# Bucketed attention and a mixture of experts on one core: 2048 instead of 16384 bytes per partition reserved for descriptors of GpSimd's DMAs

## The chip, the cores and the metric

The kernel runs on one core of a Trainium2 chip. The metric is the device time of one execution in microseconds (us), the median of several runs. A profiled execution has a span, from its first to its last recorded instruction, and a time of its own, which is a little longer.

## What is computed

Attention over 4 batches, 8 heads, 768 tokens of 64 channels, in which a query sees only the keys of its own bucket (6 sign bits of a projection), and then a mixture of 8 experts in which every token goes to the expert with the largest logit:

```python
mask = q_bucket[:, :, :, None] == k_bucket[:, :, None, :]
scores = np.where(mask, scale * np.matmul(q, k.transpose(0, 1, 3, 2)), -1000000000.0)
attn = np.exp(scores - np.max(scores, axis=-1, keepdims=True))
x = (attn / (attn.sum(-1, keepdims=True) + 1e-09)) @ v      # to 3072 rows of 512
e_idx = np.argmax(x @ w_gate, axis=1)
for e in range(8):
    mask = e_idx == e
    h = np.maximum(x[mask] @ w1[e], 0.0)                     # 512 to 1024
    out[mask] = gate_w[mask, None] * eom[mask, e, None] * (h @ w2[e])
```

All data are float32.

## The kernel before

**Attention, to about 480 us.** 192 steps, each a tile of 128 queries of one head against its 768 keys: scores on TensorE (L484), their minimum on VectorE (L488), the exponential on ScalarE (L496), the division by the row's sum on GpSimd (L506), a transpose on TensorE (L517), its eviction (L518), the product with the values (L528). The output goes to the DRAM tensor x_dram. Routing (the expert of each token and its place in a table) runs between the steps.

**Experts, from about 480 us.** The experts come in order of their load. An expert takes up to 512 tokens, in chunks of at most 128. While expert r is computed, GpSimd collects the rows of experts r+1 and r+2 by indirect DMAs: `gather` (L239) takes 128 rows of 2 KB, `gather_part` (L271) takes 128 pieces of 512 B, so that a chunk needs up to four. VectorE transposes a chunk (L280), GpSimd rounds it (L283, tile xh), VectorE forms the rest (L284, xlo). TensorE multiplies with three products for each float32 product (`product`, L297): `up` into hidden units, then `down` or, for experts with at most 384 tokens, `all_rows`. ScalarE evicts the hidden units (L307, hh), VectorE their rest (L308, hl), which frees the PSUM tile, of which there are two (ps_s).

**The way out.** `send` (L310) lets ScalarE scale a chunk of results into the tile yo (L313), of which there are two, and GpSimd scatter its rows to the output:

```python
yo = mp.tile([CH, DM], F32, name="yo", bufs=2)
nc.scalar.activation(yo[0:n], py[0:n], AF.Copy, scale=tacc[0:n, 1, r, a:a + 1])
nc.gpsimd.indirect_dma_start(
...
    in_=yo[0:n], in_offset=None, bounds_check=NTOK - 1, oob_is_err=False)
```

The order of the work on all compute engines is written out by hand (`tc.manual_schedule`): GpSimd's queue holds the gathers, the scatters and the roundings in one order, and ScalarE's queue the yo of one expert between the hh of others.

**The end.** After the last expert a number of further rounds is computed (L965 to L975), for tokens over an expert's limit; here it is 0, and the body of `tc.If(nr > 0)` (L976) is skipped. [...] The end of the tile context (profile line 1057) makes every engine's queue DRAIN, waits for all at a barrier, clears the semaphores and waits at a second barrier. In all, GpSimd issues 112 DMAs (8 by L239, 75 by L271, 29 by L314), the first at 416.6 us.

**The reservation.** The program object made at L1050 reserves, at the start of every SBUF partition, a part for the descriptors of GpSimd's DMAs, 16384 bytes if nothing is given. Tiles of pools on the left side are placed from its end on, those of pools on the right side (hp and ep) from the other end of the partition.

## Time and profile before

| | |
|---|---|
| time, median of 3 runs | 811.73 us (811.72 to 812.19) |
| time of the profiled execution | 811.82 us |
| its span | 810.1 us |
| TensorE matmul busy | 773.2 us, 95% of the span |
| GpSimd (POOL) busy | 378.4 us, 47% |
| mean granted TensorE clock | 0.986 of full speed |

A page and views of a trace are read as follows. Engines are PE (TensorE matmul), PEld (its weight loads), DVE (VectorE), ACT (ScalarE), POOL (GpSimd) and SP; a "q" behind a name is the engine's instruction queue, whose waits, branches and drains don't count as busy time. L314 is line 314 of the kernel. In a view of one line, a row gives how often an operation ran, its duration in ns (min/median/max), and when the first and the last began. In the order of time, a row gives start, duration, engine and operation, and in brackets how long the engine sat idle before it and what ended that.

### The profile page before, as it was taken

What the parts mean: (1) busy time and instruction counts of PE and PEld (TensorE: products, weight loads), DVE (VectorE), ACT (ScalarE), POOL (GpSimd) and SP (SyncE); (2) the same over time, 40 slices, a digit from 0 to 9 for tenths busy, and PEclk for the clock granted to TensorE, in tenths of its full rate; (3) what the DMA queues carried; (4) which work ended last, traced back from release to release, by engine and by line L of the source; (5) the groups of instructions that cost most, each with busy time, mean ns of one, the idle gap of its engine ahead of it and who ended that gap; (6) DMA issues with size and microseconds to landing.
All of it is one profiled execution on the core that took longest, in us unless ns stands there. A gap on an engine that the chain in (4) does not pass through costs nothing. (4 is left out here: it accounts for less than half of the span.)

```text
span 810.1 us, 13652 instructions
## 1 busy us (share of the span) xinstructions
PE 773.2 (95%) x4656; PEld 604.5 (75%) x4656; DVE 475.0 (59%) x1036; ACT 459.3 (57%) x934; POOL 378.4 (47%) x415
## 2 busy tenths in 40 slices
PE   5899999999999989999999999999999999999992
PEld 3666776666776667766667758888999999988881
DVE  5566576686667776766877637246254546455330
ACT  5767777767777677777677741243343444434320
POOL 5535444435444434443366773373436454564100
PEclk8999999999999999999999999999999999999997
DMA  3543645543564454565374432363444453645300
GB/s 122 126 119 74 146 98 121 120 123 70 136 144 87 103 140 84 121 142 131 64 204 104 115 78 46 114 222 122 137 151 146 150 175 122 222 145 182 140 15 24
DMA packets 84895, 98.94 MB, mean 122 GB/s; under 512 B 58047, under 2 KB 59535, under 8 KB 84816
## 3 DMA queue, kind: packets, MB, share of 16 engines
q1 hardware_dynamic: 79472, 84.66, 40.0%
q0 software_dynamic: 5200, 13.31, 4.9%
q8 instruction: 39, 0.64, 0.3%
q14 instruction: 40, 0.33, 0.1%
q10 hardware_dynamic: 144, 0.01, 0.0%
HBM read 59.48 MB, written 13.11 MB: 90 GB/s over the span
## 5 line engine op out<-in xcount | busy, mean ns | idle before, releaser
L506 POOL TENSOR_SCALAR sc<-sc,rsum 128x768 f32<-128x768 f32 x192 | 179.8, 948 | 234.5 <-DVE rsum L504 127.2
L488 DVE TENSOR_SCALAR_CACHE_REDUCE sc<-ps_s 128x768 f32<-128x768 f32 x192 | 183.2, 956 | 112.2 <-PE ps_s L484 104.2
L518 ACT COPY pts<-ps_t 128x384 f32<-128x384 f32 x384 | 164.4, 480 | 98.2 <-PE ps_t L517 97.4
L496 ACT ACTIVATE sc<-sc,mn 128x768 f32<-128x768 f32 x192 | 181.3, 944 | 25.8 <-DVE sc L488 16.8
L517 PE MATMUL ps_t<-ident,sc 128*128 128x128 f32 x1152 | 160.2, 275 | 6.4 <-POOL sc L506 3.8
L517 PEld LDWEIGHTS ps_t<-ident,sc 128*128 128x128 f32 x1152 | 137.3, 141 | 19.7 <-issue 6.7
L528 PE MATMUL ps_a<-pts,vt 128*64 128x384 f32 x768 | 146.4, 503 | 0.0
L484 PE MATMUL ps_s<-xr,xl 128*128 128x384 f32 x384 | 118.0, 389 | 6.2 <-DVE sc L488 3.5
L484 PEld LDWEIGHTS ps_s<-xr,xl 128*128 128x128 f32 x384 | 58.5, 192 | 78.0 <-issue 37.2
L484 PE MATMUL ps_s<-yr,yl 76*128 76x384 f32 x384 | 101.1, 344 | 0.4 <-DMA yl<-bt 0.4
L308 DVE SCALAR_TENSOR_TENSOR hl<-ps_s,hh 128x256 fp32r<-128x256 f32 (+8 forms) x40 | 33.9, 848 | 112.0 <-ACT hh L307 112.0
L297 PE MATMUL ps_s<-xh,w1h 128*128 128x256 f32 (+7 forms) x288 | 97.1, 337 | 2.0 <-DVE hl L308 1.3
L297 PE MATMUL ps_s<-xlo,w1h 128*128 128x256 f32 (+7 forms) x288 | 95.3, 331 | 0.0
L297 PE MATMUL ps_s<-xh,w1l 128*128 128x256 f32 (+7 forms) x288 | 95.2, 331 | 0.0
L271 POOL DMA_INDIRECT xq<-x_dram,idx x75 | 82.7, 1103 | 21.6 <-issue 20.7
L528 PEld LDWEIGHTS ps_a<-pts,vt 128*64 128x64 f32 x768 | 47.2, 137 | 51.6 <-issue 49.8
L314 POOL DMA_INDIRECT out_dram<-yo,sid x29 | 32.0, 1105 | 114.5 <-ACT yo L313 62.7
L307 ACT ACTIVATE hh<-ps_s 128x256 fp32r<-128x256 f32 (+8 forms) x40 | 29.0, 726 | 93.0 <-PE ps_s L297 93.0
L484 PEld LDWEIGHTS ps_s<-yr,yl 76*128 76x128 f32 x384 | 71.1, 192 | 1.1 <-DMA yl<-bt 0.7
L297 PEld LDWEIGHTS ps_s<-xh,w1h 128*128 128x128 f32 x288 | 54.1, 188 | 5.0 <-DVE hl L308 1.8
L297 PEld LDWEIGHTS ps_s<-xlo,w1h 128*128 128x128 f32 x288 | 54.1, 188 | 1.2
L297 PEld LDWEIGHTS ps_s<-xh,w1l 128*128 128x128 f32 x288 | 54.1, 188 | 1.1
(199 smaller groups left out, 1002.2 us busy)
## 6 DMA issues: line engine op xcount, KB each, us to landing
w_raw<-in_w_dram SPq DMA_DIRECT2D x36, 512.0 KB
qk<-in_qkT_dram SPq DMA_DIRECT2D x32, 384.0 KB
xh<-in_w_dram SPq DMA_DIRECT2D x14, 512.0 KB
xlo<-in_w_dram SPq DMA_DIRECT2D x14, 512.0 KB
vt<-in_v_dram SPq DMA_DIRECT2D x16, 384.0 KB
xr<-xl SPq DMA_DIRECT2D x30, 192.0 KB
yr<-xl SPq DMA_DIRECT2D x30, 192.0 KB
xr<-yl SPq DMA_DIRECT2D x30, 192.0 KB
```

Of the source, the lines that this page charges most:

```text
L271: nc.gpsimd.indirect_dma_start(out=xq[:, k * P:(k + 1) * P], out_offset=None, in_=x_dram.rearrange("n (a f) -> (n a) f", a=NB32), in_offse ...
L297: nc.tensor.matmul(ps, l, r, start=first and k == 0, stop=last and k == len(pairs) - 1)
L307: nc.scalar.activation(hh, ph, AF.Relu)
L308: return lambda: nc.vector.scalar_tensor_tensor(hl, ph, 0.0, f32(hh), ALU.max, ALU.subtract)
L314: nc.gpsimd.indirect_dma_start(out=out[:, :], out_offset=bass.IndirectOffsetOnAxis(ap=sid[0:n, r, a:a + 1], axis=0), in_=yo[0:n], in_offse ...
L484: nc.tensor.matmul(ss[:, n, 0:HS], l[0:k, qs], r[0:k, n * HS:(n + 1) * HS], start=first, stop=not first)
L488: nc.vector.tensor_scalar(sc, ss[:, :, 0:HS], MASKED, None, ALU.min, ALU.min, accum_out=mn)
L496: nc.scalar.activation(pr, pr, AF.Exp, bias=mn, scale=-1.0, accum_out=sums[s // GROUP][:, k:k + 1])
L506: nc.gpsimd.tensor_scalar(live[s0 + k], live[s0 + k], rs[:, k:k + 1], 0.0, ALU.mult, ALU.add)
L517: nc.tensor.transpose(tr[:, c], pr[:, (3 * h + c) * P:(3 * h + c + 1) * P], ident)
L518: nc.scalar.copy(pts[:, 3 * h:3 * h + 3, t * P:(t + 1) * P], tr)
L528: nc.tensor.matmul(st["av"][j * D:(j + 1) * D], st["v"][:, j, c], blocks[hb][j][:, c], start=(c == 0), stop=(c == NT - 1))
```

## The change

The reservation is given as 2048 bytes per partition.

```diff
-    nc = bacc.Bacc("TRN2", target_bir_lowering=False, num_devices=1)
+    nc = bacc.Bacc("TRN2", target_bir_lowering=False, num_devices=1, dynamic_dma_scratch_size=2048)
```

Nothing else differs. The instructions of all five engines, their order and their waits are the same. Of the tiles in SBUF, those on the left side lie 14336 bytes lower in every partition; those on the right side stay where they were.

## Rows read from the trace of the kernel before

**Rows 1.** The page: busy time of each engine, share, instructions.

```profile
PE 773.2 (95%) x4656; PEld 604.5 (75%) x4656; DVE 475.0 (59%) x1036; ACT 459.3 (57%) x934; POOL 378.4 (47%) x415
```

**Rows 2.** Busy time by stretch, first row the columns.

```profile
core 0: us, PE busy (x) PEld busy (x) DVE busy (x) ACT busy (x) POOL busy (x), PEclk, DMA share, GB/s
...
715.00:745.00 30.00, 28.72 (x149) 25.80 (x148) 15.22 (x16) 9.96 (x13) 17.93 (x17) 1.00 0.47 159
...
765.00:800.00 35.00, 30.50 (x158) 26.39 (x156) 8.29 (x8) 8.87 (x11) 3.22 (x4) 1.00 0.08 27
800.00:810.00 10.00, 0.00 (x0) 0.00 (x0) 0.00 (x0) 0.00 (x0) 0.00 (x0) 0.54 0.00 0
```

**Rows 3.** Line 1057: count, duration ns min/median/max, first and last start us.

```profile
L1057 POOLq EVENT_SEMAPHORE  x4: 17/17/17, 809.3 to 810.0; - x4
L1057 POOLq DRAIN  x3: 40/107/9226, 800.1 to 809.8; - x3
L1057 SPq DRAIN  x3: 7/7/13, 800.7 to 809.6; - x3
...
L1057 ACTq DRAIN  x2: 8/8/8, 799.0 to 809.6; - x2
```

**Rows 4.** Line 976, the skipped branch, same columns.

```profile
L976 POOLq INC_SWDGE_SEM  x1: 2418/2418/2418, 797.6 to 797.6; - x1
```

**Rows 5.** Line 1050, the program's start, same columns.

```profile
L1050 POOLq INC_SWDGE_SEM  x1: 31/31/31, 0.2 to 0.2; - x1
...
L1050 POOLq DRAIN  x1: 176/176/176, 0.4 to 0.4; - x1
```

**Rows 6.** Line 314 from 796 us on: the last scatter, and its landing.

```profile
L314 POOL DMA_INDIRECT out_dram<-yo,sid x1: 918/918/918, 796.5 to 796.5; - x1
...
DMA to landing us min/median/max: 2.8/2.8/2.8
```

**Rows 7.** Lines 239, 271, 314 over the span; the landing is line 271's.

```profile
L239 POOL DMA_INDIRECT xg<-x_dram,gid x8: 946/970/1397, 416.6 to 524.6; - x8
...
L271 POOL DMA_INDIRECT xq<-x_dram,idx x75: 940/946/1971, 525.8 to 734.4; - x75
...
DMA to landing us min/median/max: 2.4/3.2/7.0
...
L314 POOL DMA_INDIRECT out_dram<-yo,sid x29: 874/1005/1854, 506.6 to 796.5; - x29
```

**Rows 8.** POOL in order of time, from 716 us to 734 us.

```profile
716.42 0.87 POOL L314 DMA_INDIRECT out_dram<-yo,sid  x1 [1.24 <-issue]
...
731.80 0.94 POOL L271 DMA_INDIRECT xq<-x_dram,idx  x1 [0.30 <-issue]
733.05 1.03 POOL L314 DMA_INDIRECT out_dram<-yo,sid  x1 [0.30 <-issue]
```

**Rows 9.** ACT, DVE and PE in order of time, about 735 us to 739 us.

```profile
735.89 0.69 ACT L313 ACTIVATE yo<-ps_m,tacc 128x512 f32<-128x512 f32 x1 [11.75 <-DMA out_dram<-yo,sid]
736.48 0.78 ACT L307 ACTIVATE hh<-ps_s 128x736 fp32r<-128x736 f32 x1
...
737.29 0.93 DVE L308 SCALAR_TENSOR_TENSOR hl<-ps_s,hh 128x736 fp32r<-128x736 f32 x1 [11.60 <-ACT hh L307]
...
738.27 0.44 PE L297 MATMUL ps_s<-xh,w1h 128*128 128x368 f32 x1 [1.28 <-DVE hl L308]
```

**Rows 10.** POOL: its 15th DMA, and the first instructions after three runs of gathers.

```profile
530.82 0.94 POOL L271 DMA_INDIRECT xq<-x_dram,idx  x1 [0.30 <-issue]
...
557.60 0.61 POOL L283 TENSOR_SCALAR xh<-xt 128x512 fp32r<-128x512 f32 x1 [9.17 <-DVE xt L280]
...
627.21 1.48 POOL L314 DMA_INDIRECT out_dram<-yo,sid  x1 [4.01 <-ACT yo L313]
...
701.52 1.48 POOL L314 DMA_INDIRECT out_dram<-yo,sid  x1 [1.72 <-ACT yo L313]
```

**Rows 11.** Line 488 over the span: one operation on six different buffers.

```profile
L488 DVE TENSOR_SCALAR_CACHE_REDUCE sc<-ps_s x192: 944/957/960, 12.4 to 471.1; 128x768 f32<-128x768 f32 x192
```

## The prediction

> **What bounds the kernel now.** I read the page first, then busy time by stretch, then the instructions of the end by line, then the queue of POOL in order of time. TensorE is busy 95% of the span [rows 1], and its last matmul ends about 795.5 us. What follows has another limit: from 800 to 810 us no engine is busy and no DMA moves a byte [rows 2]. That is 1.2% of the run, and the busy shares of the page can't show it. The lines of the end say what fills it. The last scatter begins at 796.5 us and has landed 2.8 us later, at 799.4 us [rows 6]. POOL's queue meanwhile runs INC_SWDGE_SEM, 2.42 us from 797.6 us [rows 4], and then a DRAIN of 9.23 us from 800.1 to 809.3 us [rows 3]. ACT and SP have drained by 799.0 and 800.7 us, and their next DRAIN comes at 809.6 us, behind the barrier that POOL opens at 809.3 us [rows 3]. So the span ends as: last scatter 796.55, INC to 800.04, DRAIN to 809.29, barriers 0.82, end 810.1 us.
>
> What is the DRAIN doing for 9.9 us after the last byte has landed? The same instruction takes 176 ns at the program's start, before any DMA of POOL [rows 5], and 40 and 107 ns when it comes again right behind the long one [rows 3]. INC_SWDGE_SEM takes 31 ns at the start [rows 5] and 2,418 at the end. Between lie POOL's 112 DMAs (8 + 75 + 29) [rows 7]. My reading is that each DMA stays on a list until its space among the descriptors is wanted again, that nothing has wanted it in this run, and that the DRAIN takes 112 entries off one by one: (9,226 - 107) / 112 = 81 ns each. INC walks the same list: (2,418 - 31) / 112 = 21 ns each.
>
> **The change, part by part.**
>
> *The list becomes short.* 112 DMAs found room in 16384 bytes; an eighth of it has room for at least 112 / 8 = 14. How many more, no row says: if the old part was far from full, the list could be as long as before, so the ends are 14 and 112 entries. I take 14, the size at which the old part was just full: 112 is the only size that a row gives. [...]
>
> *INC.* Ends: 0.03 us [rows 5] and 2.42 us [rows 4]. With 14 entries 0.03 + 14 x 0.021 = 0.33 us.
>
> *DRAIN.* Call s the start of the last scatter. It holds POOL until s + 0.92; about 0.15 us of semaphore waits follow (797.47 to 797.62 now), INC to s + 1.40, and the DRAIN begins at s + 1.43. Thirteen older entries take 13 x 0.081 = 1.05 us, to s + 2.5. The last entry can't leave before it lands at s + 2.83. So what is late next is the landing: DRAIN to s + 2.91, with 0.08 us for an entry that the scatter itself had to take off first s + 2.99, and barriers of 0.82: s + 3.81. Now it is 810.11 - 796.55 = s + 13.56. **Gain 9.75 us.** If INC keeps its 2.42 us, its end is s + 3.49, fourteen entries take 1.15 us, and the end is s + 5.5: 1.7 us less gain.
>
> *Entries are taken off during the run.* From the 15th DMA on, at 530.8 us [rows 10], each needs the place of an older one: 98 removals, 8 us of POOL's time in all, if one costs what it costs in the DRAIN. The bounds: 0, if it fits into the 0.30 us of "issue" between two DMAs, and 0.30 us, if that gap doubles [rows 8]. I take 0.081, the only row with a price for it. Nothing waits for landings: 14 DMAs at 1.25 us (0.94 + 0.30) are 17.5 us, the slowest gather lands in 7.0 us [rows 7].
>
> Most of this is covered, since TensorE doesn't wait for POOL: after the runs of gathers POOL sits idle 9.2, 4.0 and 1.7 us [rows 10], and a run of 12 or 13 gathers loses about 1.0 us. One place has no cover. From 716.42 to 733.05 us POOL's queue holds 12 DMAs (two of them scatters) and one rounding without a gap but the issue time [rows 8]. Behind the last of them, a scatter that lands at about 735.8 us, ACT's yo waits 11.75 us for its buffer; behind that in ACT's queue stands hh, then hl on DVE, and TensorE stands still for 1.28 us until hl has freed the PSUM tile [rows 9]; it is all that TensorE idles from 715 to 745 us, 28.72 busy of 30 [rows 2]. Every delay of that scatter lengthens the stall one for one: 12 x 0.081 = **1.0 us lost** (bounds 0 and 3.6). TensorE has no slack behind it, so it shifts the end by as much.
>
> *Addresses.* Left-side tiles move down by 14336 bytes. No row shows a price of an address: the minimum on six buffers takes 944 to 960 ns in 192 executions [rows 11], so I cost it at nothing, with 0.5 us either way.
>
> *Sum.* 811.82 - 9.75 + 1.0 = 803.1 us against the profiled execution, whose span is 810.1; 1.7 us lie around it. The median of the runs is 0.09 us lower: **803.0 us**.
>
> **The rivals.**
>
> *The DRAIN isn't a walk over what is left* (it goes over all DMAs ever issued, or the smaller reservation leaves the list as long). For it: no row shows a removal in the run, and one long DRAIN alone can't tell entries from issues. Against: the DRAIN at 809.8 us comes after the same 112 DMAs and takes 40 ns, so what is done once is gone. Then 811.7, or 812.7 with the 1.0 us of POOL. Chance 0.07.
>
> *A list of middle length*, say 80: INC 1.7, DRAIN 6.5, end at s + 10.2, and removals begin with the 81st DMA, so the place at 716 us pays for all of its own: 811.7 - 3.4 + 1.0 = 809 us. Chance 0.05.
>
> *Slower: POOL waits for space.* If the small part holds only one or two DMAs, each waits until an earlier one has landed. It decides from the point where the list holds fewer than 3.2 / 1.25 = 2.6 DMAs at the median landing [rows 7]. Then a gather takes 3.2 us instead of 1.25, the 12 DMAs at 716 us cost 12 x 1.95 = 23 us in the stall, and with the gain at the end the time is at least 811.7 - 9.75 + 23 = 825 us; other runs of gathers would outgrow their idle time too. Against it stands the eighth of 112. [...] Chance 0.05.
>
> **How the numbers follow.** The forecast has the remaining 0.83. Its own bounds: no price on POOL gives 802.0, with 0.5 for addresses 801.5; removals at 0.30 us and an unchanged INC give 803.0 + 2.6 + 1.7 = 807.3. Removals beyond 0.2 us I hold unlikely, so the range is 801.5 to 807.0, which leaves out about 2 in 10: the three rivals and the corners. A measurement of this kernel tells 0.2% (1.6 us) from no change. Faster: 0.83 + 0.05 = 0.88. Within 0.2%: the first rival, 0.07. Slower: 0.05.
>
> **What would show it.** Right: POOL's DRAIN at line 1057 between 0.5 and 2 us, INC at line 976 under 0.6 us, the barriers 0.1 us behind the last landing; DMAs of line 271 from the fifth gather on some 80 ns longer, or their issue gap; the stall of TensorE near 738 us at about 2.3 us instead of 1.28. Wrong: a DRAIN of 9 us again (first rival), one of several us (second), gathers of 2 us and more without DVE's work beside them (third). If the stall at 738 us is unchanged, the removals are free and the time is 802. The prediction falls if the time is over 807.0.

## The result, and the profile after

| | before | after |
|---|---|---|
| time, median of 4 runs each (us) | 811.73 (810.57 to 812.19) | 802.62 (801.96 to 803.36) |
| ratio, 95% interval | | 0.989 (0.9873 to 0.9907) |
| profiled execution: time / span (us) | 811.82 / 810.1 | 803.36 / 801.6 |
| last scatter starts / has landed (us) | 796.55 / 799.38 | 797.13 / 800.20 |
| INC_SWDGE_SEM of POOL's queue (ns) | 2,418 | 458 |
| long DRAIN of POOL's queue (ns) | 9,226 | 2,116 |
| behind the last landing, to the end of the span (us) | 10.73 | 1.45 |

The change is 9.1 us faster, and 803.0 us (801.5 to 807.0) had been predicted. The end of the program first, as it now is: line 1057, the end of the tile context, in the columns of [rows 3].

```profile
L1057 SPq EVENT_SEMAPHORE  x14: 17/28/30291, 768.3 to 801.6; - x14
L1057 POOLq EVENT_SEMAPHORE  x4: 17/17/17, 800.9 to 801.5; - x4
L1057 POOLq DRAIN  x3: 40/107/2116, 798.7 to 801.4; - x3
L1057 SPq DRAIN  x3: 7/7/13, 800.8 to 801.1; - x3
```

And line 976, the skipped branch, in the same columns:

```profile
L976 POOLq INC_SWDGE_SEM  x1: 458/458/458, 798.2 to 798.2; - x1
```

Against [rows 3] and [rows 4]: the two shorter DRAINs of POOL still take 40 and 107 ns, the long one has lost 7.11 us and INC 1.96 us. Before, SP had drained at 800.7 us and waited for POOL until 809.3; now both are done at 800.8. From the last scatter's start to the end of the span it is 4.52 us instead of 13.56, a gain of 9.04 us. The last scatter begins 0.58 us later than before, so that 8.46 us are left between the two profiled executions. Busy time by stretch, the columns of [rows 2], shows that nothing else moved much:

```profile
715.00:745.00 30.00, 28.43 (x147) 25.48 (x146) 14.93 (x15) 10.24 (x13) 17.95 (x17) 1.00 0.46 154
765.00:800.00 35.00, 31.07 (x161) 26.98 (x160) 8.29 (x8) 8.87 (x11) 3.84 (x4) 0.98 0.08 28
```

The other rows that the prediction named are those of POOL's queue from 716 us on, the answer to [rows 8]:

```profile
716.98 0.88 POOL L314 DMA_INDIRECT out_dram<-yo,sid  x1 [1.50 <-issue]
718.16 1.01 POOL L271 DMA_INDIRECT xq<-x_dram,idx  x1 [0.31 <-issue]
...
732.36 0.96 POOL L271 DMA_INDIRECT xq<-x_dram,idx  x1 [0.30 <-issue]
733.62 1.03 POOL L314 DMA_INDIRECT out_dram<-yo,sid  x1 [0.30 <-issue]
```

The same DMAs and the rounding between these two scatters take 733.62 - 716.98 = 16.64 us; before they took 733.05 - 716.42 = 16.63. By the theory every DMA of this stretch needs the place of an older one, and between these two scatters that costs nothing that can be seen. The gap ahead of the first of them did grow: POOL sat idle 1.50 us there, before 1.24 [rows 8]. That is 0.27 us by the trace, and the sizes below show where it comes from. ACT and TensorE behind it, the answer to [rows 9]:

```profile
736.47 0.69 ACT L313 ACTIVATE yo<-ps_m,tacc 128x512 f32<-128x512 f32 x1 [12.03 <-DMA out_dram<-yo,sid]
737.05 0.77 ACT L307 ACTIVATE hh<-ps_s 128x736 fp32r<-128x736 f32 x1
...
738.84 0.44 PE L297 MATMUL ps_s<-xh,w1h 128*128 128x368 f32 x1 [1.57 <-DVE hl L308]
```

From the scatter's start to yo it is 2.85 us, before 2.84. The stall is 1.57 us instead of 1.28, about as much longer as that gap, and not the 2.3 us that were predicted.

### The profile page after: what moved, and what is told of

Its sections match the earlier page's. It is cut to its first block, busy times and chain, and to the rows that moved or that the text cites. A ratio compares the mean times of both kernels' runs of the same rounds, so it can differ in the third digit from the quotient of the medians.

```text
span 801.6 us, 13652 instructions
## 1 busy us (share of the span) xinstructions
PE 776.2 (97%) x4656; PEld 606.2 (76%) x4656; DVE 472.6 (59%) x1036; ACT 459.1 (57%) x934; POOL 375.9 (47%) x415
## 5 line engine op out<-in xcount | busy, mean ns | idle before, releaser
L528 PE MATMUL ps_a<-pts,vt 128*64 128x384 f32 x768 | 148.6, 510 | 0.0
L314 POOL DMA_INDIRECT out_dram<-yo,sid x29 | 30.6, 1057 | 115.3 <-ACT yo L313 61.3
```

Source lines behind the costliest of these rows:

```text
L314: nc.gpsimd.indirect_dma_start(out=out[:, :], out_offset=bass.IndirectOffsetOnAxis(ap=sid[0:n, r, a:a + 1], axis=0), in_=yo[0:n], in_offse ...
L528: nc.tensor.matmul(st["av"][j * D:(j + 1) * D], st["v"][:, j, c], blocks[hb][j][:, c], start=(c == 0), stop=(c == NT - 1))
```

## The experiments

The theory at this point: INC and the DRAIN walk over the DMAs of POOL that are still listed, at about 20 and 82 ns each; the size of the reservation sets how many are listed. The rivals: the DRAIN became short for another reason (bytes to be cleared, the tiles' new addresses), or the list is freed in another way than one entry for one DMA.

### Four other sizes

The edit, the number being 12288, 6144, 1024 and 320 in turn:

```diff
-    ... dynamic_dma_scratch_size=2048)
+    ... dynamic_dma_scratch_size=12288)
```

**12288 bytes.** 

> The part has 12288 bytes, three quarters of the old one. Theory (a list from which the oldest entry is taken off when its place is wanted): room for 85 DMAs, so 85 entries at the end; INC_SWDGE_SEM 0.18 + 85 x 0.020 = 1.9 us, DRAIN 85 x 0.081 = 6.9 us, a time near 809 us. Rival A (when the part is full the whole list is cleared): 112 - 85 = 27 entries, INC 0.7 us, DRAIN 2.2 us, a time near 803 us. Rival B (the DRAIN counts DMAs issued, or the short time comes from the addresses and any other size gives it): DRAIN 9.2 us or 2.1 us.

**6144 bytes.** 

> The part has 6144 bytes. Theory (oldest entry goes when its place is wanted): 42 entries at the end, INC 0.18 + 42 x 0.020 = 1.0 us, DRAIN 42 x 0.081 = 3.4 us, a time near 805 us. Rival A (the whole list is cleared when the part is full): 112 - 84 = 28 entries, INC 0.7 us, DRAIN 2.3 us. Rival B as in the run with 12288 bytes.

**1024 bytes.** 

> The part has 1024 bytes, room for 7 DMAs. Theory: 7 entries at the end, INC 0.18 + 7 x 0.020 = 0.32 us; the DRAIN ends as late after the last landing as with 2048 bytes (0.6 us), since the landing and SP's own waits bound it, so the time is that of 2048 bytes within 0.3 us, gathers still 1.25 us apart. Rival (waits for space grow steadily as the part shrinks): gathers more than 1.3 us apart and a longer stall near 738 us.

**320 bytes.** 

> The part has 320 bytes, room for two DMAs. Theory: below 3.2 / 1.25 = 2.6 DMAs POOL must wait for landings. With two in flight a gather can start when the last but one has landed: start to start (3.2 + 0.3) / 2 to 3.2 us instead of 1.25, so the 12 DMAs before 733 us take 6 to 23 us longer, the stall near 738 us grows by as much, and the time is 808 to 835 us. Rival (space is never waited for, the part is only an address): no difference from 2048 bytes.

Measured in one profiled execution each, all in us but the last column. The rows of 16384 and 2048 bytes are those of the result; on the chip of the other four the kernel before took 811.51 us. The tail is the time from the last landing to the end of the span, and the entries are worked out below:

| bytes | time | last scatter at | INC | long DRAIN | DRAIN's end behind the landing | tail | entries |
|---|---|---|---|---|---|---|---|
| 16384 | 811.82 | 796.55 | 2.418 | 9.226 | 9.91 | 10.73 | 112 |
| 12288 | 801.66 | 794.41 | 0.838 | 2.774 | 1.81 | 2.64 | 33 |
| 6144 | 803.72 | 795.74 | 0.978 | 3.346 | 2.28 | 3.10 | 40 |
| 2048 | 803.36 | 797.13 | 0.458 | 2.116 | 0.63 | 1.45 | 14 |
| 1024 | 802.50 | 796.43 | 0.318 | 1.800 | 0.34 | 1.45 | 7 |
| 320 | 825.39 | 819.02 | 0.225 | 1.994 | 0.14 | 1.45 | 2 |

Lines 976 and 1057 of the kernel with 12288 bytes, where the count went wrong:

```profile
L976 POOLq INC_SWDGE_SEM  x1: 838/838/838, 795.5 to 795.5; - x1
...
L1057 POOLq DRAIN  x3: 40/107/2774, 796.4 to 799.7; - x3
```

the same lines of the one with 6144:

```profile
L976 POOLq INC_SWDGE_SEM  x1: 978/978/978, 796.8 to 796.8; - x1
...
L1057 POOLq DRAIN  x3: 40/107/3346, 797.8 to 801.7; - x3
```

and of the one with 1024:

```profile
L976 POOLq INC_SWDGE_SEM  x1: 318/318/318, 797.5 to 797.5; - x1
...
L1057 POOLq DRAIN  x3: 40/107/1800, 797.9 to 800.5; - x3
```

*What a walk costs.* Take 112 entries for 16384 bytes and 14 for 2048, as predicted: then INC's price is (2,418 - 458) / 98 = 20.0 ns an entry, with 178 ns of its own. Half the bytes of 2048 should leave 7, and 178 + 7 x 20 = 318 ns is what 1024 bytes show to the nanosecond. So the same line may be read backwards: 978 ns are 40 entries and 838 are 33. The 225 ns of 320 bytes are 2 entries and 7 ns more. The DRAIN is a second witness that was not used in this. From 40 to 112 entries it grows by (9,226 - 3,346) / 72 = 81.7 ns an entry, and 33 entries then give 3,346 - 7 x 81.7 = 2,774 ns, again the measured number. That 12288 bytes have a shorter DRAIN than 6144, 2,774 ns against 3,346, also rules out that it clears bytes. At 14 entries and fewer the DRAIN is longer than its entries at this price (2,116 ns where 14 make 1,144) and ends 0.63 to 0.14 us behind the last landing: I take it to wait for that, so its duration is no longer a count.

*What a smaller part does to the list.* Here my theory fell. If a full list gave up one entry for each new DMA, 12288 bytes, three quarters of the old part, would hold 84 or more at the end; the INC would be near 1.9 us and the time 809 us. It held 33. (The 85 places written beforehand are the number of no run; three quarters of 112 are 84.) If the list was full at 84, the last 112 - 84 = 28 DMAs came after, so no more than 5 of the earlier ones were still on it: on this count many entries went at once. By which rule stays open; clearing all of them would leave 28 with either size. With its 33 entries 12288 bytes bring nearly the whole gain: a tail of 2.64 us instead of 10.73.

*What making room costs.* If 112 DMAs just fill 16384 bytes, 6144 have 112 x 6144 / 16384 = 42 places, an estimate. The 43rd DMA of POOL, a scatter, would be the first that finds them taken. In the kernel before it stands in POOL's order of time as

```profile
603.60 0.94 POOL L314 DMA_INDIRECT out_dram<-yo,sid  x1 [1.29 <-ACT w1h L162]
```

with 6144 bytes as

```profile
603.87 0.94 POOL L314 DMA_INDIRECT out_dram<-yo,sid  x1 [2.23 <-issue]
```

and with 2048 as

```profile
604.63 0.94 POOL L314 DMA_INDIRECT out_dram<-yo,sid  x1 [1.57 <-issue]
```

The idle time ahead of it is 0.94 us longer with 42 places and 0.28 us longer with 14. The 92nd DMA, the scatter at 716 us, shows the same: 1.50 to 1.52 us of idle time in all seven profiled executions with 2048 bytes (the experiments below included), 1.35 and 1.38 us with 1024 and 320 bytes, and 1.23 to 1.24 us in all five with 6144 or more. The longer wait comes with the smaller part and not with the addresses, since the tile that puts them back (below) leaves it at 1.50. So making room is not free: it is paid ahead of single DMAs, 0.27 us once before the stretch from 716 to 733 us, and not 0.08 us for each DMA in it. That POOL clears a batch of entries in these gaps fits the sizes and is not shown.

*What is late next.* 2048, 1024 and 320 bytes all end 1.45 us behind the last landing, though POOL's DRAIN ends 0.63, 0.34 and 0.14 us behind it. With 1024 and 320 bytes another queue has taken over. The waits of SP's queue from 690 us on in the kernel after show which:

```profile
engine line waited for: us in total, times, longest us
SPq L1057 <- DMA out_dram<-yo,sid: 35.5, 2, 34.1
...
SPq L1057 <- PEq L1057: 0.7, 2, 0.5
```

SP waits at line 1057 for a row of semaphores one behind the other, the last scatter's among them, and the trace has eight more behind it, some 60 ns apart though nothing holds them up any more. Its first DRAIN at that line starts 0.57 us behind the landing in all three kernels, and the barriers follow. With 2048 bytes the two queues are level: POOL's 0.63 us and the 0.82 us from the end of its DRAIN to the end of the span, the same as before, also make 1.45. A still shorter list, of 7 or 2 entries, has gained nothing at this end.

*When the part is too small.* At 320 bytes the prediction's slower rival comes true. POOL's queue over the stretch that takes 16.64 us with 2048 bytes:

```profile
732.11 0.88 POOL L314 DMA_INDIRECT out_dram<-yo,sid  x1 [1.38 <-issue]
...
740.25 1.96 POOL L271 DMA_INDIRECT xq<-x_dram,idx  x1 [0.30 <-issue]
744.45 0.95 POOL L271 DMA_INDIRECT xq<-x_dram,idx  x1 [2.24 <-issue]
747.60 0.94 POOL L271 DMA_INDIRECT xq<-x_dram,idx  x1 [2.19 <-issue]
...
753.59 1.03 POOL L314 DMA_INDIRECT out_dram<-yo,sid  x1 [0.84 <-issue]
```

It takes 753.59 - 732.11 = 21.48 us here. The idle time before a gather is no longer always 0.30 us but up to 2.24, with no releaser that the profile knows. Whom that stops is in TensorE's waits of the same kernel from 520 to 765 us:

```profile
PE ps_s L297 <- DVE hl L308: 8.2, 3, 7.5
PE ps_m L297 <- ACT yo L313: 4.2, 1, 4.2
PE ps_s L297 <- ACT hh L307: 2.7, 1, 2.7
```

and in its busy time by stretch:

```profile
520.00:765.00 245.00, 228.47 (x1185) 213.13 (x1184) 109.95 (x112) 87.75 (x106) 120.54 (x116) 0.97 0.44 143
```

The same stretch in the kernel after the change:

```profile
520.00:765.00 245.00, 242.84 (x1289) 226.60 (x1288) 121.13 (x126) 94.50 (x114) 120.22 (x121) 1.00 0.48 159
```

TensorE loses 242.84 - 228.47 = 14.4 us of busy time, and its granted clock is 0.97 instead of 1.00 besides. The stall behind the stretch is 7.5 us, 5.9 longer than with 2048 bytes; the rest is lost at other places, as the waits show. The time is 825.39 us, 13.9 over the kernel before on that chip (811.51). The point from which waiting decides lies between 2 and 7 entries, where the prediction had 2.6.

### The walk moved, and the bytes left at 16384

If the gain is the list alone, it must come without any change of the reservation: let POOL walk the list where it has nothing to do. Before the last expert is computed:

```diff
+            if r == E - 1:
+                nc.gpsimd.drain()
```

on the kernel before. 

> The kernel before with its 16384 bytes, and one more drain of POOL's queue ahead of the last expert (about 765 us), where POOL has some 20 us without work. Theory (the end pays for the entries that are still listed, whatever the size of the part): the added DRAIN takes 0.08 + 109 x 0.082 = 9.0 us beside TensorE's work; at the end 3 entries are left, INC 0.18 + 3 x 0.020 = 0.24 us, the last DRAIN ends 0.1 to 0.2 us after the last landing, and the time is that of 2048 bytes, 801 to 804 us. Rival (the small part or the moved addresses give the gain): 811 to 812 us.

This and the first runs of the three kernels below were on a second chip, where the kernel before took 815.85 us (813.94 to 818.59, 11 runs). The times in us that were expected for them had been written from the result, where the kernel before is 4 us faster, so the ratios decide. The time was 807.74 us, ratio 0.9893 (0.9867 to 0.9919), that of the change in the result. The new line (two lines added, so 1057 and 976 are now 1059 and 978):

```profile
L919 POOLq DRAIN  x1: 10168/10168/10168, 768.9 to 768.9; - x1
```

The closing DRAINs of the same kernel:

```profile
L1059 POOLq DRAIN  x3: 46/107/1854, 802.7 to 805.6; - x3
```

its INC:

```profile
L978 POOLq INC_SWDGE_SEM  x1: 256/256/256, 802.5 to 802.5; - x1
```

and POOL there in the order of time:

```profile
769.16 0.95 POOL L314 DMA_INDIRECT out_dram<-yo,sid  x1 [3.02 <-ACT yo L313]
790.29 0.99 POOL L314 DMA_INDIRECT out_dram<-yo,sid  x1 [20.19 <-ACT yo L313]
```

The added DRAIN starts in the queue at 768.92 us, while the scatter of 769.16 us is still to come, and ends at 779.09. From that scatter's end at 770.10 us it is 8.99 us, and 109 entries at 81.7 ns with 80 ns besides are 8.98. It lies in a hole of 20.19 us between two scatters, in which POOL waits for ACT's yo anyway. At the end three scatters are left on the list; INC takes 256 ns, and the tail is 1.47 us. So neither bytes nor addresses are needed for the gain: it is the list at the end. The entries can also be taken off earlier, at no cost that this measurement can tell from none.

These three entries also check the count without the assumption that 2048 bytes leave 14. INC of the kernel with 16384 bytes and a third yo buffer (below), where all 112 are left:

```profile
L976 POOLq INC_SWDGE_SEM  x1: 2436/2436/2436, 800.0 to 800.0; - x1
```

and of the change on the second chip:

```profile
L976 POOLq INC_SWDGE_SEM  x1: 476/476/476, 807.3 to 807.3; - x1
```

From 3 to 112 entries it is (2,436 - 256) / 109 = 20.0 ns an entry, so 476 ns are 3 + (476 - 256) / 20.0 = 14 entries. On these two chips INC takes 18 ns more at 14 and at 112 entries than in the table above.

### The addresses

The change with a tile of 14336 bytes at the start of the left side, so that every tile lies where it lay before (and one memset of a column more on POOL):

```diff
+    pad = cst.tile([P, 3584], F32, name="pad")
+    nc.gpsimd.memset(pad[:, 0:1], 0.0)
```

> 2048 bytes, and a tile of 14336 bytes ahead of all others, so that the tiles lie where they lay before. Theory (addresses cost nothing): the time of the change, 801 to 804 us, INC 0.46 us, DRAIN about 2.1 us. Rival (part of the gain comes from the addresses): over 805 us.

Beside it the change once more, without an edit. 

> The changed kernel once more, beside the others on the same chip: 802.0 to 803.4 us; its stall near 738 us tells how much of the 0.29 us that it grew by (1.28 to 1.57) comes back. Theory (removals cost POOL nothing that is seen): anything between 0.8 and 1.6 us. Rival (removals delay the scatter before the stall): 1.5 us or more again.

The first gave 807.76 us, ratio 0.9908 (0.9882 to 0.9934), the second 810.3 us, 0.9925 (0.9899 to 0.995). Both end 1.45 us behind the last landing. The change gained only 5.6 us here, against 9.1 in the result, with the same tail; what it lost elsewhere was not followed up beyond the profile shown at the end of the next section. Its stall was 2.91 us, which by what was written beforehand speaks for the rival, that removals delay the scatter ahead of it. The change was the slower of the two by 2.5 us, though the intervals overlap; so both ran again on a third chip, in six runs each. The pad again: 

> The change with every left-side tile at its old address. If addresses cost nothing, equal to after3 within 0.1%. If the lower addresses cost something, under after3 by more than 1 us.

The change again: 

> The change itself, for comparison on this chip: ratio 0.988 to 0.991, INC about 0.46 us, DRAIN about 2 us.

There the kernel before took 816.76 us (812.65 to 819.32, 17 runs), the pad 808.39 us, 0.9904 (0.9875 to 0.9933), and the change 807.65 us, 0.9885 (0.986 to 0.991). The sign has turned, and each lies in the other's interval. No price of the addresses shows; 0.3% of the time, the half-width of these intervals, is how much could be hidden.

### A third yo buffer

What the prediction called the one place without cover, the stall near 738 us, comes from ACT's yo, which waits for one of two buffers. The change with a third:

```diff
-        yo = mp.tile([CH, DM], F32, name="yo", bufs=2)
+        yo = mp.tile([CH, DM], F32, name="yo", bufs=3)
```

> The change, and three tiles yo where there were two (2 KB more per partition, of the 14 KB set free). Theory (the stall of TensorE near 738 us comes from ScalarE's wait for a tile yo): no stall of hl there, 0.85 to 1.57 us less than the change, a time of 801 to 801.8 us. Rival (another wait stands right behind it): the stall stays, no gain.

On the second chip 804.16 us, ratio 0.9858 (0.9835 to 0.988), with 0.9925 for the change without it; a stall of 0.48 us was left at that place. Then on the third chip the same kernel again, 

> The change with the third yo buffer once more. If the third buffer is worth what the stall held, 1 to 2 us under after3 and a ratio to before of 0.986 to 0.988. If its lead in the earlier run was the scatter of that chip, it equals after3.

and the third buffer on the kernel before, with 16384 bytes: 

> The kernel before with a third yo buffer. If the stall of TensorE near 738 us comes from the yo that waits for its buffer alone, the stall falls from 1.28 us to about 0.5 us (as in yo3) and the time lies 0.8 to 1.5 us under the kernel before, ratio 0.998 to 0.999; the end stays as before, INC 2.4 us and DRAIN 9.2 us, so that the two gains add: change 9 us, third buffer about 1 us. If yo3 owed its lead over the other 2048-byte kernels to the reservation's smaller part, this kernel equals the kernel before.

| third chip | time (us) | ratio to before (95%) | tail (us) |
|---|---|---|---|
| before | 816.76 | 1 | |
| before with a third yo | 813.58 | 0.996 (0.9944 to 0.9976) | 10.39 |
| the change | 807.65 | 0.9885 (0.986 to 0.991) | 1.45 |
| the change with a third yo | 805.0 | 0.9855 (0.9833 to 0.9878) | 1.45 |

The last is the fastest kernel of the study. The two gains add: 3.2 us by the buffer without the change, 2.7 with it; 9.1 us by the change without the buffer, 8.6 with it. ACT of this fastest kernel (its run on the third chip) in the order of time:

```profile
727.82 0.69 ACT L313 ACTIVATE yo<-ps_a,tacc 128x512 f32<-128x512 f32 x1 [2.99 <-issue]
733.38 0.69 ACT L313 ACTIVATE yo<-ps_m,tacc 128x512 f32<-128x512 f32 x1 [4.87 <-PE ps_m L297]
737.36 0.79 ACT L307 ACTIVATE hh<-ps_s 128x736 fp32r<-128x736 f32 x1 [3.29 <-issue]
```

yo no longer waits 12 us for a scatter but 4.87 us for TensorE, its own source, and hh begins at 737.36, 3.29 us behind it instead of at its heels. Busy time by stretch of that kernel:

```profile
715.00:745.00 30.00, 30.00 (x154) 26.70 (x153) 13.15 (x14) 11.35 (x14) 19.75 (x18) 1.00 0.47 157
```

and of the change on the same chip:

```profile
715.00:745.00 30.00, 28.39 (x143) 24.79 (x142) 12.21 (x13) 9.65 (x12) 19.50 (x19) 1.00 0.40 143
```

The stall of 30.00 - 28.39 = 1.61 us is gone; with 16384 bytes and the third buffer 0.55 us of it is left. But the buffer's gain, 2 to 4.6 us by the interval, is more than the 0.8 to 1.5 us that I expected. One profiled execution shows one way in which it might be. In the second profile of the change, on the second chip, the stall was 2.91 us, and busy time by stretch around it reads:

```profile
746.40:747.90 1.50, 1.43 (x8) 1.43 (x9) 1.49 (x3) 1.50 (x2) 0.00 (x0) 0.99 0.43 175
747.90:751.30 3.40, 3.40 (x14) 3.40 (x12) 3.40 (x4) 2.01 (x3) 1.04 (x1) 0.50 0.73 219
751.30:753.00 1.70, 1.70 (x12) 1.70 (x12) 0.59 (x1) 0.66 (x1) 0.00 (x0) 1.00 0.90 330
```

TensorE stood still until 746.47 us, worked at a granted clock of 0.99 up to 747.9, and then for 3.4 us at 0.50. Its matmuls of 128x368 begin 0.31 us apart there (748.24, 748.54, 748.85 us), before it 0.17 (747.07, 747.24, 747.41): an estimate from this is that 3.4 us hold the work of 1.9. The early drain's profile has the same fall, from 741.9 us on (0.78 in the mean of 738 to 745 us), behind a stall of 1.88 us; the pad's on the third chip has none (1.00 from 738 to 752 us) behind a stall of 2.71 us. So a stall may cost more than its length, but not each does, and that the stall brings the fall is argued from two profiles. Whether this makes up the rest of the buffer's gain was not tried.

## Why the prediction was right, and where it was not

The prediction's steps one by one, against the profiled execution of the change:

- **What bounds the end.** Right: the gap of 10 us was the walk of POOL's DRAIN and INC over DMAs long done. It was argued from two rows; sizes from 1024 to 16384 bytes and the early drain now show it, 8.99 us for 109 entries where 8.98 were expected by the price.
- **The list becomes short, 14 entries.** Right in number. The picture behind it, one out for one in, is refuted by 12288 bytes; the rival of a middle-length list falls with INC's 458 ns. That 14 came out is no proof of the rule by which entries go: 112 is a multiple of 14, 7 and 2, so a list that is cleared whole each time it is full would end with the same numbers.
- **INC, 0.33 us.** Measured 0.458. The price of an entry was 20 ns, as said, but the part that doesn't depend on the list is 178 ns, not the 31 of [rows 5].
- **The DRAIN and the barriers, to s + 3.81 us.** The order was right, the landing binds; measured s + 4.52. Of the 0.71 us missing, 0.24 is a landing that took 3.07 us instead of 2.83. The other 0.47 is the way from the landing to the end, 1.45 us instead of 0.98: I had 0.16 us behind the landing, where POOL's DRAIN ends 0.63 behind it, and I had left out SP's row of waits, which alone would take 0.57. The barriers, 0.82 us, were right. The DRAIN of 2.12 us also lies just outside the 0.5 to 2 us that I had named as a sign. POOL's 0.63, 0.34 and 0.14 us at 14, 7 and 2 entries grow by some 41 ns an entry, half of the 81.7: as if half of each entry's walk came behind the last landing. The early drain's three entries, 0.17 us, lie near that line. This reading is argued from four numbers and not shown.
- **"Entries are taken off during the run": 1.0 us lost at the place without cover.** This is the step that failed. It took the DRAIN's 81 ns as the price of an entry in the run, on the ground that no other row had a price. The stretch at 716 us has the same length to 0.01 us, and the gap between two gathers is 0.30 us before [rows 8] and after; neither the gathers nor their gaps are 80 ns longer. What grew is the one gap ahead of the stretch's first scatter, by 0.27 us, in every execution with 2048 bytes. So the loss at this place was about 0.3 us instead of 1.0: the price is not one of each DMA. That entries leave in batches would explain it and is not shown.
- **The stall at 2.3 us.** 1.57 us. With two yo buffers and 2048 bytes the other four profiles have 1.61, 1.63, 2.71 and 2.91. With 16384, 12288, 6144 and 1024 bytes it is 1.28, 0.85, 0.96 and 1.26 on the chips of the result and the sizes, but 1.88 with 16384 bytes and the early drain on the second chip. That agrees with a loss of some 0.3 us, and the scatter of one kernel is larger than that.
- **Addresses, 0 with 0.5 us either way.** Nothing shown against it; the runs bound it only to some 0.3%.
- **The sum.** 803.1 us was forecast for the profiled execution, 803.36 came. Two errors hide in this closeness. The tail gained 13.56 - 4.52 = 9.04 us instead of 9.75, and the last scatter began 0.58 us later than before instead of 1.0. Of those 0.58 us only the 0.27 of the gap before 716.98 us come with the smaller part. The rest was there earlier: the gather at 527 us was 0.22 us late (527.29 after 527.07), before the 15th DMA was due, and the scatter before the gap 0.30 us. In the kernels with 12288, 6144 and 1024 bytes the last scatter began at 794.41 to 796.43 us. So that the sum came out to 0.3 us is luck.

Of the rivals, the first (no walk) fell by every size, the second (80 entries) was not met, and the third (POOL waits for space) was met with 320 bytes, a sixth of this part, where POOL sat idle in that stretch for up to 2.24 us ahead of a gather, and not with 1024 (802.50 us). That its price came out, at least 825 us written and 825.39 measured, is luck: it put 23 us into the stall behind 733 us, which grew by 6.2 us over that of before, the stretch by 4.8. The rest was lost at other runs of gathers and by the lower clock, 0.97 from 520 to 765 us.

## What to carry to other kernels

Look at what the queues do after the last byte has landed: busy shares don't show it, since a DRAIN doesn't count as work, and here it was 1.2% of the time. Here the end of the program paid 102 ns for each DMA of GpSimd that was still listed (81.7 in the DRAIN from 40 to 112 entries, 20.0 in INC). A reservation of 2048 bytes took 9.1 us away, and a drain of GpSimd in a hole of its own earlier on as much by the ratio (0.9893, against 0.989); with 320 bytes, 2 entries, the kernel took 13.9 us more than before. A cost that a row showed at one place (81 ns for an entry in the closing DRAIN) was not the price of the same thing elsewhere (16.64 us for a stretch of DMAs that took 16.63). And where a cost is looked for in a stretch, look at the gap ahead of its first instruction too: here it was there.

## What the runs showed that I had not expected

- A part a quarter smaller leaves not 84 but 33 entries, and half of that smaller part, 6144 bytes, leaves more, 40. My reading is that many go at once when there is no more room, and that what is left at the end depends on where in that cycle the program stops; how entries go was not shown.
- At most of the DMAs for which room had to be made nothing of it shows: the gap between two gathers stayed 0.30 us. It shows as 0.27 us ahead of single scatters, whereas the same entries cost 102 ns each at the end (81.7 in the DRAIN, 20 in INC).
- A queue of waits that were all satisfied still took time here: some 60 ns each on SP (eight from 800.3 to 800.7 us). With the barriers that makes 1.45 us, and no kernel of this study ended closer behind its last landing.
